# An FNet and SwiGLU block on one core: modulation's sums rearranged, one row block's load moved, and the last but one group's second products in seven instead of eight

## The chip, the core and the metric

The kernel runs on one core of a Trainium2 chip. The time is the device time of one execution, in microseconds (us). A run gives the median of several executions; beside it there is one profiled execution with a trace of each engine: TensorE (PE, its weight loads PEld), VectorE (DVE), ScalarE (ACT), GpSimd (POOL) and SyncE (SP).

## The reference

A row block of 2048 rows by 512 columns goes through a Fourier mixing layer and then a gated feed-forward layer, each behind a layer norm that is modulated by a conditioning vector c:

```python
mod = (_silu(c) @ w_mod).reshape(c.shape[0], 6, 1, -1)
sa, ca, ga, sb, cb, gb = (mod[:, 0], mod[:, 1], mod[:, 2], mod[:, 3], mod[:, 4], mod[:, 5])
h = _layernorm(x, axis=-1) * (1 + ca) + sa
x = x + ga * _A_ref(h, A_dft_seq_re, A_dft_seq_im, A_dft_hid_re, A_dft_hid_im)
h = _layernorm(x, axis=-1) * (1 + cb) + sb
x = x + gb * _B_ref(h, B_w1, B_w3, B_w2)
# _A_ref: y = Cr @ (h Wr) - Ci @ (h Wi);  _B_ref: (silu(h w1) * (h w3)) w2
```

## The kernel before

All matmuls on float32 data are made of splits: a tile is rounded to a high part (a copy on ScalarE), the rest is its low part (a subtraction on VectorE), and a product is three matmuls (high by high, high by low, low by high). `product` does these three.

**The start.** ScalarE and SP issue the first loads. The sums sa and ca of modulation come from `mod_scale` and `mod_sum`: the four parts of w_mod for one vector (tiles `wmr`; `wm[v, h][:, n]`, v = 1 for ca, 0 for sa) are scaled by silu(c) and added up on VectorE, the first of them scaled by ScalarE (`copy_by`), and four small matmuls by ones (`mod_sum`) sum them over the partitions. `mod_read` takes them out of PSUM, and then `modulate_rows` (tile `hm`) can begin on the first row block, which has been normalized (`norm_stats`, `norm_root` with a square root on ScalarE, `norm_inverse`, `norm_scale`) and transposed (`turn_rows`) by then. `keep_warm` issues matmuls that nobody reads; 25 of them stand between the last sum and the first real product. After the start, `arrange` orders tasks by a table of ranks and times, until the products over the sequence (line 750) begin.

**The feed-forward part.** The 1792 columns in the middle are seven groups g of 256, and the four column blocks t of 512 rows are two pairs: pair 0 is t = 0 and 2, pair 1 is t = 1 and 3. The products by w1 (called a) and w3 (called b) of one group and pair are done by Strassen's method in Winograd's form: seven units, a1 to a7 and b1 to b7 (`factor`), of six matmuls of 512 columns. From them come `v` = silu(a) times b and its split `hf`. The second products, by w2 (called y in the program's string of the order), are spread between the a and b units of the next group. For the groups in the list `SEVEN`, 0 to 4 of pair 1, they too are seven units (`seven_unit`, in the order 2, 5, 3, 1, 6, 7, 4), of six matmuls in two PSUM banks, 6 and 7; units 3, 6, 7 and 4 add to the banks of the unit before them, so each unit's banks have to be read before the next unit with the same banks begins. ScalarE reads them (`copy_by`, line 335, tile `y`, scaled by gb), and a transfer that POOL issues adds `y` (512 KB) to `sums` in DRAM. Such groups also need the sums of w2's quarters and their splits (`seven_jobs`: tiles `w2s`, `w2sh`, `w2sl`) and four differences of `v` (`seven_parts`). All other groups have eight units of six matmuls (`down_unit`).

Groups 5 and 6 of pair 1 come last. Their eight units each are `own`: VectorE adds the bank, scaled by gb, to the tile `xr` (line 1147), which `load_sums` has loaded from `sums` after group 4; after group 6 the result goes from `xr` to the output. Here `down_banks` are 6, 7, 0, 1 and 2 in turn. The order of the last units is a string, `body`, for each group; `behind(n, ...)` puts the splits some units later, `delayed` issues them ahead of a unit. Everything an engine gets, it does in the order of the program.

Of the kernel before, what the change touches and what calls it, by code (L numbers as in the profile page):

```python
# [12 lines left out]
OP = mybir.AluOpType  # L13
AX = mybir.AxisListType

P = 128
# [5 lines left out]
NT = S // N  # L22
ND = D // P
# [19 lines left out]
def folded(nc, pools, c, cp, wmr, wmc, x, xt, ctr, cti, wdr, wdi, w1, w3, w2, out):  # L43
# [155 lines left out]

    held = consts.tile([1, 1], F32, name="held")  # L200

    def load_x(k, other=nc.sync):
        if k >= NK // 2:
            nc.gpsimd.tensor_copy(held, wd[0][0:1, 1, 0:1].bitcast(F32))


        i, par = where(k)
        xz[k] = take(F32, "x")
        nc.sync.dma_start(xz[k][:, 0, :], x[i][par::2])
        if par:  # L210
# [27 lines left out]
    load_wm(0, 1, nc.sync)  # L238
    for dt in range(2):
        load_hid(dt, nc.sync)  # L240
    load_x(1)
    for dt in range(2, ND):
        load_hid(dt, nc.sync)
    for k in range(2, 4):
# [53 lines left out]

    mod_acc = [bank(5), bank(6)]

    def mod_scale(v, h):

        w, own = wm[v, 0][:, 0, :], wm[v, h]
        if h == 0:
            copy_by(w, w, sc[:, 0:1])
        for n in range(1 - h, 2):
            nc.vector.scalar_tensor_tensor(
                w, own[:, n, :], sc[:, 2 * h + n : 2 * h + n + 1], w, op0=OP.mult, op1=OP.add
            )

    def mod_sum(v):

        for dt in range(ND):
            nc.tensor.matmul(
                mod_acc[v][:, cols(dt)],
                hid_cols(wm[v, 0][:, 0, :], dt),
                onesf[:, :P],
                start=True,
                stop=True,
            )  # L320

    def mod_read(v):
# [11 lines left out]
    def copy_by(dst, src, by):  # L334
        nc.scalar.activation(dst, src, AF.Identity, scale=by)  # L335
# [789 lines left out]
    def down_unit(g, pair, t, d, key):  # L1125
        last = g == NG - 1

        own = pair == 1 and g >= NG - 2
        if not own and d % 2 == 0:
            ys[0] = take(F32, "y")  # L1130

        parts = 2 if own and last and (t, d) == (NT - 1, ND - 1) else 1
# [32 lines left out]
        if d == ND - 1:  # L1165
            for q in range(2):
                give(hf.pop((g, t, q)))
            if t == PAIRS[pair][1]:
                give_w(key)
            if pair == 1 and g == NG - 3:  # L1170
                load_sums(t)
# [51 lines left out]
    TO = {1: 0, 6: 0, 7: 0, 4: 0, 2: 1, 5: 2, 3: 2}  # L1223
    state, vs = {}, {}

    SEVEN = [(g, 1) for g in range(NG - 2)]
    ORDER7 = (2, 5, 3, 1, 6, 7, 4)
    LEFT7 = {1: "h0", 2: "h2", 4: "h3", 5: "s0", 6: "s1", 7: "s2", 3: "s3"}
    TO7 = {2: (0, 0), 5: (1, 1), 3: (0, 1), 1: (0, 0), 6: (0, 1), 7: (1, 1), 4: (1, 0)}
# [101 lines left out]
    def seven_unit(g, pair, n, key):  # L1331
        new = n in (1, 2, 5)
        if new:
            banks7[:] = [bank(6), bank(7)]
        y = take(F32, "y")
        which, k = TO7[n]
        t = PAIRS[pair][k]
        names = ("h", "l") if LEFT7[n][0] == "h" else ("sh", "sl")
        u = right7.pop(((g, pair), n))
        for e, to in enumerate(banks7):  # L1340
            at = int(LEFT7[n][1]) * HALF + e * P
            product(
                to,
                [flat(wuse[key][x])[:, at : at + P] for x in names],
                [u[:, b, :] for b in range(2)],
                new,
                True,
                not new,
            )
            d = 2 * which + e  # L1350
            copy_by(y[:, e, :], to, gb[:, d : d + 1])
        give(u)
        nc.gpsimd.dma_start(sums[t, which], y, accum_op=OP.add)  # L1353
        behind(4, lambda: give(y))
        if n == ORDER7[-1]:
            for x in wuse.pop(key).values():
                give(x)
            if g == NG - 3:
                for t in PAIRS[pair]:
                    load_sums(t)  # L1360
# [134 lines left out]
    }  # L1495
    seq_steps = []
    keep_warm(3)
    for side in range(2):
        norm_stats(0, side)
    norm_root(0)  # L1500
    norm_inverse(0)
    for side in range(2):
        norm_scale(0, side, "ACT" if side else "DVE")
        turn_rows(0, side)
    keep_warm(1)
    for v, h in ((1, 0), (1, 1), (0, 0)):
        mod_scale(v, h)
    mod_sum(1)
    copy(nought, zero[:, 0, :P])
    clear_z()  # L1510
    hid_begin(0)
    keep_warm(6, P)
    mod_scale(0, 1)
    mod_read(1)
    mod_sum(0)
    mod_read(0)


    at(10.0, "turn0.0", "turn0.1")
# [184 lines left out]
    def down(g, pair, *which):  # L1704
        key = which[-1]
        drain(lambda: (key, "l") in done, jobs)
        delayed()
        if (g, pair) in SEVEN:
            seven_unit(g, pair, *which)
        else:  # L1710
            down_unit(g, pair, *which)
        beside(1.36, USED["own" if pair == 1 and g >= NG - 2 else "y"])

    for w in ("w1", "w3"):
        load_w((w, 1))
# [36 lines left out]
    def unit(kind, i, n):  # L1752
# [23 lines left out]
        if (kind, n) == ("b", 3):  # L1776
# [9 lines left out]
            if (g, pair) in SEVEN:  # L1786
                seconds.extend((g, pair, n, ("w2", g, pair)) for n in ORDER7)
            else:
                for t in PAIRS[pair]:
                    seconds.extend((g, pair, t, d, ("w2", g, pair)) for d in range(ND))  # L1790
# [7 lines left out]
    for i in range(len(items)):  # L1798
# [834 lines left out]
```

## Time and profile before

| | us |
|---|---|
| median of 3 runs (lowest, highest) | 692.39 (691.91, 694.4) |
| the profiled execution: its own time | 690.63 |
| its span, first to last instruction | 688.8 |
| TensorE busy | 672.4 |
| VectorE busy | 586.8 |
| ScalarE busy | 451.2 |

A row of a timeline gives start and duration in us, the engine, the source line, the operation, the tile written and the tiles read, the shape and a count; in brackets stand the engine's idle time before it and what ended that. Times are from the first instruction. L335 is ScalarE's scaled copy, L100 a matmul of `product`, L87 a copy on ScalarE, L90, L93 and L96 VectorE's subtraction, addition and multiplication.

### The profile page before, as it was taken

What the parts mean: (1) busy time and instruction counts of PE and PEld (TensorE: products, weight loads), DVE (VectorE), ACT (ScalarE), POOL (GpSimd) and SP (SyncE); (2) the same over time, 40 slices, a digit from 0 to 9 for tenths busy, and PEclk for the clock granted to TensorE, in tenths of its full rate; (3) what the DMA queues carried; (4) which work ended last, traced back from release to release, by engine and by line L of the source; (5) the groups of instructions that cost most, each with busy time, mean ns of one, the idle gap of its engine ahead of it and who ended that gap; (6) DMA issues with size and microseconds to landing.
All of it is one profiled execution on the core that took longest, in us unless ns stands there. A gap on an engine that the chain in (4) does not pass through costs nothing.

```text
span 688.8 us, 9035 instructions
## 1 busy us (share of the span) xinstructions
PE 672.4 (98%) x3122; PEld 557.4 (81%) x3122; DVE 586.8 (85%) x945; ACT 451.2 (65%) x751; POOL 132.2 (19%) x156
## 2 busy tenths in 40 slices
PE   6999999999999999999999999999999999999996
PEld 4898788888888888888788888887887888888785
DVE  5999769998999987989997989787998979888465
ACT  4998956455343665663577767867687887877620
POOL 1320162543435000100101001011011112221100
PEclk9999999999999999999999999999999999999998
DMA  8740299787679440274767666475859998999713
GB/s 264 224 124 1 54 368 339 249 297 258 197 287 291 154 151 30 46 139 122 119 141 141 150 153 121 94 128 118 267 108 183 175 203 167 181 214 173 179 45 127
DMA packets 40837, 116.80 MB, mean 170 GB/s; under 512 B 5200, under 2 KB 5456, under 8 KB 40784
## 3 DMA queue, kind: packets, MB, share of 16 engines
q0 software_dynamic: 14512, 50.86, 36.9%
q1 hardware_dynamic: 25840, 63.98, 28.1%
q10 hardware_dynamic: 432, 1.31, 0.6%
q8 instruction: 26, 0.43, 0.3%
q14 instruction: 27, 0.22, 0.1%
HBM read 76.81 MB, written 41.42 MB: 172 GB/s over the span
## 4 chain that ended last, share of the span: by engine, by line
PE 84%; DVE 9%; ACT 4%; issue 1%; DMA 1%; SPq 0%; DVEq 0%; ACTq 0%
PE bank L100 54%; PE bank L750 26%; PE bank L559 2%; PE bank L598 1%; ACT hm L501 1%; DMA x<-in_x 1%; DVE xr L806 1%; DVE st L449 1%; PE bank L576 1%; DVE v L96 1%; DVE hl L90 0%; DVE ul L90 0%; DVE x L93 0%; ACT hh L87 0%; DVE w3s L90 0%
## 5 line engine op out<-in xcount | busy, mean ns | idle before, releaser
L100 PE MATMUL bank<-hf,w2h 128*128 128x512 f32 (+1 forms) x352 | 108.3, 389 | 0.0
L87 ACT ACTIVATE hf<-v 128x512 fp32r<-128x512 f32 x71 | 44.4, 631 | 66.7 <-DVE v L96 53.9
L335 ACT ACTIVATE y<-bank,gb 128x512 f32<-128x512 f32 x118 | 76.5, 682 | 3.9 <-PE bank L100 3.6
L100 PEld LDWEIGHTS bank<-hf,w2h 128*128 128x128 f32 x352 | 65.6, 188 | 15.4 <-ACT y L335 1.5
L1161 POOL DMA_DIRECT2D sum<-y x28 | 24.0, 857 | 240.7 <-ACT y L335 124.5
L100 PE MATMUL bank<-hf,w2l 128*128 128x512 f32 (+1 forms) x176 | 68.1, 387 | 0.0
L90 DVE TENSOR_TENSOR hf<-v,hf 128x512 fp32r<-128x512 f32 x71 | 48.7, 685 | 10.6 <-ACT hf L87 10.5
L1353 POOL DMA_DIRECT2D sum<-y x35 | 29.8, 852 | 128.3 <-ACT y L335 120.8
L87 ACT ACTIVATE x<-bank 128x512 f32<-128x512 f32 x72 | 41.7, 591 | 13.6 <-PE bank L100 12.7
L750 PE MATMUL bank<-d,uh 128*128 128x512 f32 x128 | 49.9, 390 | 0.0
L750 PE MATMUL bank<-l,us 128*128 128x512 f32 x128 | 49.9, 390 | 0.0
L750 PE MATMUL bank<-d,us 128*128 128x512 f32 x128 | 49.9, 390 | 0.0
L750 PE MATMUL bank<-bh,us 128*128 128x512 f32 x128 | 49.9, 390 | 0.0
L750 PE MATMUL bank<-bh,ul 128*128 128x512 f32 x128 | 49.8, 389 | 0.0
L750 PE MATMUL bank<-l,uh 128*128 128x512 f32 x128 | 49.8, 389 | 0.0
L170 POOL DMA_INDIRECT re<-in_ctr,mirror x32 | 35.7, 1115 | 66.6 <-ACT im L188 40.1
L170 POOL DMA_INDIRECT im<-in_cti,mirror x32 | 32.9, 1028 | 33.4 <-DVE l L90 8.9
L100 PEld LDWEIGHTS bank<-hf,w2l 128*128 128x128 f32 x176 | 33.1, 188 | 6.6
L93 DVE TENSOR_TENSOR v<-bank,x 128x512 f32<-128x512 f32 x36 | 24.7, 686 | 15.6 <-PE bank L100 14.0
L1245 ACT ACTIVATE v<-v 128x512 f32<-128x512 f32 x36 | 22.6, 629 | 22.7 <-DVE v L93 22.4
L93 DVE TENSOR_TENSOR x<-bank,x 128x512 f32<-128x512 f32 x36 | 24.7, 685 | 14.5 <-PE bank L100 13.7
L188 ACT ACTIVATE im<-l 128x512 f32<-128x512 f32 x16 | 10.1, 632 | 32.4 <-DVE d L93 15.5
(260 smaller groups left out, 1922.4 us busy)
## 6 DMA issues: line engine op xcount, KB each, us to landing
sum<-y POOLq DMA_DIRECT2D x63, 512.0 KB, 5.7
w<-in_w SPq DMA_DIRECT2D x42, 512.0 KB, 4.8
re<-in_ctr SPq DMA_DIRECT2D x32, 256.0 KB, 5.8
im<-in_cti SPq DMA_DIRECT2D x32, 256.0 KB, 5.3
wmc<-in_wmc SPq DMA_DIRECT2D x8, 512.0 KB, 7.2
sum<-xr SPq DMA_DIRECT2D x8, 512.0 KB, 5.6
x<-in_x SPq DMA_DIRECT2D x11, 256.0 KB, 4.5
xr<-in_xt SPq DMA_DIRECT2D x8, 256.0 KB, 7.1
```

Of the source, the lines that this page charges most:

```text
L87: nc.scalar.activation(dst, src, AF.Copy, scale=scale)
L90: nc.vector.tensor_tensor(out=dst, in0=a, in1=b, op=OP.subtract)
L93: nc.vector.tensor_tensor(out=dst, in0=a, in1=b, op=OP.add)
L100: nc.tensor.matmul(acc, lhs[a], rhs[b], start=first and n == 0, stop=last and n == len(PASSES) - 1, skip_group_check=more,)
L170: nc.gpsimd.indirect_dma_start(dst, None, rows, bass.IndirectOffsetOnAxis(ap=at, axis=0))
L188: nc.scalar.activation(to, src.bitcast(F32), AF.Square, accum_out=chk[:, kind, KINDS.index(m), n : n + 1],)
L335: nc.scalar.activation(dst, src, AF.Identity, scale=by)
L559: nc.tensor.matmul(halves(hb[k])[:, m, :], sides((hh, hl)[a][k])[:, dt, m, :], wu[dt][:, b, m, :], start=False, stop=dt % 2 == 1 and n == ...
L750: nc.tensor.matmul(acc[what, e], lhs, rhs, start=begin and i == 0, stop=(end or (turn and what == "x")) and i == len(terms) - 1, skip_grou ...
L1161: nc.gpsimd.dma_start(sums[t, d // 2], y, accum_op=OP.add)
L1245: behind(k != 0 or q == 0, lambda: nc.scalar.activation(v, src, AF.Silu))
L1353: nc.gpsimd.dma_start(sums[t, which], y, accum_op=OP.add)
```

## The change

Three things are changed. At the start, ca's first copy and first add, and the zeroing copies, stand ahead of the layer norm's square root and its scaling; sa is summed in two parts, by two sets of four matmuls that add up in PSUM, with a matmul by zeros ahead of them to set the bank to zero (`mod_begin`), so that one add on VectorE is replaced by a copy on ScalarE. Second, the load of row block 1 is issued by ScalarE, behind the scaled copies, and not by SP. Third, group 5 of pair 1 joins `SEVEN`: its second products are seven units that are read by ScalarE and added by transfers, to `xr` in SBUF; the string of the last group's order is adapted, and the last group's eight units take the places of t = 3 ahead of the last two of t = 1.

```diff
@@ load_x and the first loads
-    def load_x(k, other=nc.sync):
+    def load_x(k, other=nc.sync, one=nc.sync):
...
-        nc.sync.dma_start(xz[k][:, 0, :], x[i][par::2])
+        one.dma_start(xz[k][:, 0, :], x[i][par::2])
...
-    load_x(1)
@@ modulation
-    def mod_scale(v, h):
-
-        w, own = wm[v, 0][:, 0, :], wm[v, h]
-        if h == 0:
-            copy_by(w, w, sc[:, 0:1])
-        for n in range(1 - h, 2):
-            nc.vector.scalar_tensor_tensor(
-                w, own[:, n, :], sc[:, 2 * h + n : 2 * h + n + 1], w, op0=OP.mult, op1=OP.add
-            )
+    def mod_copy(v, h, n):
+        w = wm[v, h][:, n, :]
+        copy_by(w, w, sc[:, 2 * h + n : 2 * h + n + 1])
+
+    def mod_add(v, h, n):
+        w, own = wm[v, 0][:, 0, :], wm[v, h]
+        nc.vector.scalar_tensor_tensor(
+            w, own[:, n, :], sc[:, 2 * h + n : 2 * h + n + 1], w, op0=OP.mult, op1=OP.add
+        )
+
+    def mod_begin():
+        nc.tensor.matmul(
+            mod_acc[0], zero[:, 0, :P], onesf, start=True, stop=False, skip_group_check=True
+        )
...
-    def mod_sum(v):
+    def mod_sum(v, h=0, apart=False):
...
-                hid_cols(wm[v, 0][:, 0, :], dt),
+                hid_cols(wm[v, h][:, 0, :], dt),
                 onesf[:, :P],
-                start=True,
-                stop=True,
+                start=not apart,
+                stop=not apart or h == 0,
+                skip_group_check=apart,
@@ the start's order
     keep_warm(3)
+    copy(nought, zero[:, 0, :P])
+    clear_z()
     for side in range(2):
         norm_stats(0, side)
+    mod_copy(1, 0, 0)
     norm_root(0)
+    mod_add(1, 0, 1)
     norm_inverse(0)
...
-    keep_warm(1)
-    for v, h in ((1, 0), (1, 1), (0, 0)):
-        mod_scale(v, h)
+    mod_begin()
+    mod_add(1, 1, 0)
+    mod_copy(0, 0, 0)
+    mod_add(1, 1, 1)
+    mod_copy(0, 1, 0)
+    load_x(1, nc.scalar, nc.scalar)
     mod_sum(1)
-    copy(nought, zero[:, 0, :P])
-    clear_z()
+    mod_add(0, 0, 1)
+    mod_sum(0, 1, True)
+    mod_add(0, 1, 1)
+    keep_warm(1, P)
+    mod_sum(0, 0, True)
+    mod_read(1)
+    mod_read(0)
     hid_begin(0)
-    keep_warm(6, P)
-    mod_scale(0, 1)
-    mod_read(1)
-    mod_sum(0)
-    mod_read(0)
@@ the second products
-        own = pair == 1 and g >= NG - 2
+        own = pair == 1 and g == NG - 1
...
-    SEVEN = [(g, 1) for g in range(NG - 2)]
+    SEVEN = [(g, 1) for g in range(NG - 1)]
...
-        nc.gpsimd.dma_start(sums[t, which], y, accum_op=OP.add)
+        to = xr[t][which] if g == NG - 2 else sums[t, which]
+        nc.gpsimd.dma_start(to, y, accum_op=OP.add)
...
+                if not more:
+                    places = places[:2] + places[4:] + places[2:4]
...
-            body = "a6 a5 b1 a7 a3 b2 a4 y b6 y b5 y b7 y b4 y y b3 y y y y y y y y y y"
+            body = "a6 a5 b1 a7 a3 b2 y a4 y b6 y b5 y b7 y b4 y b3 y y y y y y y y y"
```

How the change moves instructions is shown at three places; after a name stand a bank's or buffer's number and a counter.

**ScalarE at the start**, before: silu(c) (`sc`), the square root (`rs`) with its table load, the scaling of the first row block's second half, and two scaled copies.

```order
L286 ACT_TABLE_LOAD
L286 ACTIVATE sc_145<-cc_84 128x4
L454 ACT_TABLE_LOAD
L454 ACTIVATE rs_0_162<-mv_0_161,eps_128 128x2
L468 ACTIVATE x_1_87<-x_1_87,rs_0_162 128x512
L335 ACTIVATE wmr_2_90<-wmr_2_90,sc_145 128x512
L335 ACTIVATE wmr_4_94<-wmr_4_94,sc_145 128x512
L87 ACTIVATE nought_155<-zero_13_140 128x128
```

The same place of ScalarE after the change:

```order
L285 ACT_TABLE_LOAD
L285 ACTIVATE sc_142<-cc_84 128x4
L87 ACTIVATE nought_152<-zero_12_137 128x128
L87 ACTIVATE z_17_153<-zero_12_137 128x1024
L340 ACTIVATE wmr_2_90<-wmr_2_90,sc_142 128x512
L459 ACT_TABLE_LOAD
L459 ACTIVATE rs_0_161<-mv_0_160,eps_125 128x2
L473 ACTIVATE x_1_87<-x_1_87,rs_0_161 128x512
L340 ACTIVATE wmr_4_94<-wmr_4_94,sc_142 128x512
L340 ACTIVATE wmr_5_96<-wmr_5_96,sc_142 128x512
L209 DMA x_20_190<-in_x 128x1x512
L211 DMA x_20_190<-in_x 128x1x512
```

The second table load and the square root now stand behind the first scaled copy, and two DMA issues behind the last.

**ScalarE where group 5's b units end and group 6's a units begin**, before: w3sh is the high part of group 6's w3 sums, hf_960 a split of group 5's v, the y are evictions of group 4's units, x_963 and v_964 results of a1 and a2.

```order
L87 ACTIVATE w3sh_956_5829<-w3s_951_5809 128x1024
L87 ACTIVATE x_958_5838<-bank5_957_5831 128x512
L87 ACTIVATE hf_960_5850<-v_916_5606 128x512
L335 ACTIVATE y_961_5852<-bank6_952_5815,gb_152 128x512
L335 ACTIVATE y_961_5852<-bank7_953_5816,gb_152 128x512
L87 ACTIVATE x_963_5870<-bank0_962_5863 128x512
L1245 ACTIVATE v_964_5871<-v_964_5871 128x512
L335 ACTIVATE y_968_5885<-bank6_952_5815,gb_152 128x512
```

After the change ScalarE has there:

```order
L87 ACTIVATE x_958_5837<-bank5_957_5830 128x512
L87 ACTIVATE hf_960_5852<-v_916_5605 128x512
L340 ACTIVATE y_961_5854<-bank6_952_5814,gb_149 128x512
L340 ACTIVATE y_961_5854<-bank7_953_5815,gb_149 128x512
L87 ACTIVATE w3sh_963_5866<-w3s_959_5839 128x1024
L87 ACTIVATE x_965_5876<-bank0_964_5869 128x512
L1251 ACTIVATE v_966_5877<-v_966_5877 128x512
L340 ACTIVATE y_971_5893<-bank6_952_5814,gb_149 128x512
```

w3sh has moved from ahead of hf_960 to behind the two y. VectorE, after the change, has at the same place (w3l and w3sl are the low parts of group 6's w3 and of its sums; the rows ahead of these are the sums and splits of w2, which are new):

```order
L90 TENSOR_TENSOR w3s_959_5839<-w3_934_5728,w3s_959_5839 128x256
L93 TENSOR_TENSOR x_958_5837<-bank3_943_5765,x_958_5837 128x512
L96 TENSOR_TENSOR v_916_5605<-v_916_5605,x_958_5837 128x512
L90 TENSOR_TENSOR w3l_962_5864<-w3_934_5728,w3h_956_5828 128x1024
L90 TENSOR_TENSOR hf_960_5852<-v_916_5605,hf_960_5852 128x512
L90 TENSOR_TENSOR w3sl_969_5882<-w3s_959_5839,w3sh_963_5866 128x1024
L93 TENSOR_TENSOR v_966_5877<-bank1_970_5884,x_965_5876 128x512
```

Before, w3l and w3sl stood ahead of x_958 and v_916; now they stand behind them, and w3sl ahead of v_966.

**ScalarE and TensorE at the end.** The last activations of ScalarE were, before, an x and three splits hf; after the change they are:

```order
L87 ACTIVATE hf_1004_6109<-v_967_5878 128x512
L340 ACTIVATE y_1005_6111<-bank6_999_6069,gb_149 128x512
L340 ACTIVATE y_1005_6111<-bank7_1000_6070,gb_149 128x512
L87 ACTIVATE hf_1006_6150<-v_966_5877 128x512
L340 ACTIVATE y_1007_6152<-bank6_999_6069,gb_149 128x512
L340 ACTIVATE y_1007_6152<-bank7_1000_6070,gb_149 128x512
```

hf_1006 is the split of the v that b3 ends, y_1007 the eviction of unit 4. TensorE's unit 4 and the first unit of the last group stand so after the change:

```order
L100 MATMUL bank6_999_6069<-hf_985_5991,w2h_947_5793 128x512 x2
L100 MATMUL bank6_999_6069<-hf_985_5991,w2l_950_5809 128x512
L100 MATMUL bank7_1000_6070<-hf_985_5991,w2h_947_5793 128x512 x2
L100 MATMUL bank7_1000_6070<-hf_985_5991,w2l_950_5809 128x512
L100 MATMUL bank7_1008_6163<-hf_989_6008,w2h_987_6003 128x512 x2
L100 MATMUL bank7_1008_6163<-hf_989_6008,w2l_988_6005 128x512
```

bank7_1000 and bank7_1008 are the same PSUM bank, one after the other.

More of the change, by code (lines that the diff above doesn't have):

```diff
@@ L1126, in down_unit @@
         last = g == NG - 1
-        own = pair == 1 and g >= NG - 2
+        own = pair == 1 and g == NG - 1
         if not own and d % 2 == 0:
             ys[0] = take(F32, "y")
-        parts = 2 if own and last and (t, d) == (NT - 1, ND - 1) else 1
+        final = (t, d) == ((PAIRS[1][0] if own else PAIRS[pair][1]), ND - 1)
+        parts = 2 if own and final else 1
         for n in range(parts):
@@ L1167, in down_unit @@
                 give(hf.pop((g, t, q)))
-            if t == PAIRS[pair][1]:
+            if final:
                 give_w(key)
@@ L1711, in down @@
             down_unit(g, pair, *which)
-        beside(1.36, USED["own" if pair == 1 and g >= NG - 2 else "y"])
+        beside(1.36, USED["own" if pair == 1 and g == NG - 1 else "y"])
     for w in ("w1", "w3"):
@@ L1788, in unit @@
             else:
-                for t in PAIRS[pair]:
-                    seconds.extend((g, pair, t, d, ("w2", g, pair)) for d in range(ND))
+                t0, t1 = PAIRS[pair]
+                places = [(t, d) for t in (t0, t1) for d in range(ND)]
+                if not more:
+                    places = places[:2] + places[4:] + places[2:4]
+                seconds.extend((g, pair, t, d, ("w2", g, pair)) for t, d in places)
         if (kind, n) == ("b", 6) and more and early_w3(i):
```

## The prediction

> **What bounds the kernel now.** First the busy shares and the chain of work that ended last.
>
> ```profile
> PE 672.4 (98%) x3122; PEld 557.4 (81%) x3122; DVE 586.8 (85%) x945; ACT 451.2 (65%) x751; POOL 132.2 (19%) x156
> PE 84%; DVE 9%; ACT 4%; issue 1%; DMA 1%; SPq 0%; DVEq 0%; ACTq 0%
> 86.65 174.32 PE bank L750 x768
> ```
>
> TensorE is busy for 98% of the span and is 84% of the chain; from 86.65 us on the chain is TensorE alone for 174 us. So what counts is TensorE's issue time: matmuls taken out of it, and waits put into it. Other engines matter only in the first 86 us, where the chain runs through them, and where TensorE waits for them. The timeline of TensorE late in the program gives the pace:
>
> ```profile
> 639.40 0.39 PE L100 MATMUL bank<-th,w3h 128*128 128x512 f32 x1
> 640.53 0.39 PE L100 MATMUL bank<-th,w3l 128*128 128x512 f32 x1
> 640.93 0.73 PE L100 MATMUL bank<-hf,w2h 128*128 128x512 f32 x2
> 642.42 0.39 PE L100 MATMUL bank<-h2h,w3sh 128*128 128x512 f32 x1
> ```
>
> The first and sixth matmul of one unit start 1.13 us apart, so a matmul costs 0.226 us and a unit of six 1.36 us (its listed 0.39 us is overlapped). The next unit could have begun at 640.76; it began 0.17 late, and took 1.49 us: a restart after a wait costs another 0.13. That is a second product waiting for its bank, and the point that the change presses on.
>
> **The start.** Its rows, from the timeline and (the second one) the DMA issues:
>
> ```profile
> 1.41 1.16 ACTq L220 DMA_DIRECT2D wmr<-in_wmr  x2
> wmr<-in_wmr ACTq DMA_DIRECT2D x2, 512.0 KB, 6.9
> 2.60 4.51 PE L281 MATMUL bank<-tmp 128*128 128x512 f32 x6 [2.60 <-DVE tmp L275]
> 2.61 1.28 ACT L286 ACT_TABLE_LOAD   x1 [2.61 <-issue]
> 3.90 0.20 ACT L286 ACTIVATE sc<-cc 128x4 f32<-128x4 f32 x1
> 4.12 1.28 ACT L454 ACT_TABLE_LOAD   x1
> 7.50 0.30 ACT L454 ACTIVATE rs<-mv,eps 128x2 f32<-128x2 f32 x1 [2.09 <-DVE mv L450]
> 8.23 0.55 DVE L470 TENSOR_SCALAR x<-x,rs 128x512 f32<-128x512 f32 x1
> 9.95 1.02 PE L281 MATMUL bank<-tmp 128*128 128x512 f32 x2
> 10.07 0.72 ACT L335 ACTIVATE wmr<-wmr,sc 128x512 f32<-128x512 f32 x1 [0.42 <-DMA wmr<-in_wmr]
> 10.47 1.54 DVE L307 SCALAR_TENSOR_TENSOR wmr<-wmr,sc,wmr 128x512 f32<-128x512 f32 x2
> 12.06 1.21 PE L314 MATMUL bank<-tmp,wmr 128*128 128x128 f32 x8 [1.09 <-DVE wmr L307]
> 13.03 0.48 PE L549 MATMUL bank<-z,nought 128*128 128x512 f32 x1
> 15.62 5.75 PE L281 MATMUL bank<-tmp 128*128 128x128 f32 x50
> 16.02 1.02 ACT L501 ACTIVATE hm<-bank,mod 128x256 f32<-128x256 f32 x2 [1.94 <-DVE mod L324]
> 21.82 0.51 PE L559 MATMUL bank<-wu,hh 128*128 128x256 f32 x2 [0.45 <-ACT hh L87]
> ```
>
> Before, ScalarE loads the Sqrt table at 4.12, in idle time. Now the table load stands behind the first scaled copy of w_mod, and that copy waits for its DMA. The two ScalarE DMAs took 6.9 us on average; the second, issued at about 2.0, ended the copy's wait at 10.07, so took 8.0; the first then took 5.8 and landed at 1.41 + 5.8 = 7.2. Copy 0.72, table load 1.28: Sqrt at 9.2 instead of 7.50, **1.7 us later**. VectorE's scaling starts 0.73 after Sqrt (8.23 - 7.50): 9.93, ends 10.48. Now only two adds (0.77 each, 1.54 for two) stand before the first sum: 12.02, and TensorE starts it at 12.07, where it started before (12.06). What was gained by moving adds forward is spent on the table load.
>
> From there TensorE sets the pace. One sum takes 0.97 (12.06 to 13.03). Before, the two sums with the product by zeros and 12 filler passes between them ended at 15.62, where the 50 passes begin. Now come three sums and one filler matmul (two passes of 5.75/50): 12.07 + 3 x 0.97 + 0.23 = 15.21. VectorE's last two adds end at 12.02 + 1.54 = 13.56, under that. The mod values, and so hm on ScalarE, come **0.41 us sooner** (15.6 for 16.02). The 25 filler matmuls then end at 15.21 + 0.23 (the product by zeros) + 5.75 = 21.2, and the first real product is due at 21.82 - 0.41 = 21.41: they still fit. Beyond it the order of all engines up to the last two groups is as before, and no load stands on the chain there, so I carry the 0.41 to 86.65 and to the end. Its ends: 0 (absorbed on the way), and 2.1, if the table load cost nothing (1.7 more). The second row block's two DMA issues now cost ScalarE 1.16 (as at 1.41), between the copies' end at about 12.0 and hm at 15.6, where two casts of 0.42 are all else: covered. If that cover went, hm would be late by the rest of 1.16. SP is free of them; nothing was seen waiting for SP's loads of the third and fourth weight part, so I count nothing.
>
> The Trainium skill, ScalarE: Activation LUTs, What ACT_TABLE_LOAD costs, adds a drain of 1.38 us to each switch of 1.28. Here the load at 2.61 ends at 3.89 and the next activation starts at 3.90: the trace shows no drain. By the page Sqrt would come at 10.6 and the start would lose about 1.0 instead of gaining 0.41, and the sum below would be 4.5 instead of 3.15.
>
> **The last two groups.** Removed: 48 matmuls become 42, 6 x 0.226 = **-1.36 us**. Also removed are eight VectorE additions from PSUM; added are 14 ScalarE evictions, seven POOL transfers into xr, splits and sums of w2, and four differences. None of these is on TensorE's path by itself; what matters is where TensorE waits for an eviction. I follow three places.
>
> ```profile
> 630.87 0.42 DVE L93 TENSOR_TENSOR w3s<-w 128x256 f32<-128x256 f32 x1
> 632.33 0.68 DVE L90 TENSOR_TENSOR hf<-v,hf 128x512 fp32r<-128x512 f32 x1
> 632.93 1.21 DVE L90 TENSOR_TENSOR w3l<-w,w3h 128x1024 fp32r<-128x1024 f32 x1
> 634.07 1.22 DVE L90 TENSOR_TENSOR w3sl<-w3s,w3sh 128x1024 fp32r<-128x1024 f32 x1
> 635.92 0.69 DVE L96 TENSOR_TENSOR v<-v,x 128x512 f32<-128x512 f32 x1
> 632.95 1.06 ACT L87 ACTIVATE w3sh<-w3s 128x1024 fp32r<-128x1024 f32 x1
> 636.64 0.63 ACT L87 ACTIVATE hf<-v 128x512 fp32r<-128x512 f32 x1 [2.15 <-DVE v L96]
> 637.18 1.25 ACT L335 ACTIVATE y<-bank,gb 128x512 f32<-128x512 f32 x2
> 638.32 0.59 ACT L87 ACTIVATE x<-bank 128x512 f32<-128x512 f32 x1
> 638.95 0.69 DVE L93 TENSOR_TENSOR v<-bank,x 128x512 f32<-128x512 f32 x1 [0.95 <-ACT x L87]
> 639.67 0.63 ACT L1245 ACTIVATE v<-v 128x512 f32<-128x512 f32 x1 [0.76 <-DVE v L93]
> 640.21 1.25 ACT L335 ACTIVATE y<-bank,gb 128x512 f32<-128x512 f32 x2
> ```
>
> *First wait, at 640.93.* Ahead of the v at 635.92, VectorE loses w3l and w3sl (2 x 1.14, from 632.93 to 634.07) and gains the four w2 sums (1.46, as 630.87 to 632.33) and w2sl (1.14): v comes 0.32 later, at 636.24, and ends at 636.94; hf on ScalarE at 636.97, y y at 637.51. Behind them now stands w3sh, which stood ahead before: 638.65 to 639.71. VectorE's w3sl waits for it: 639.74, and the v of 638.95 is queued behind w3sl (1.14): 640.88. Silu follows 0.72 later (639.67 - 638.95): 641.60, y y 0.54 later: 642.14, and TensorE 0.72 after that (640.93 - 640.21): 642.86. **+1.92 us.** Its ends: 0.32 if the wait for w3sh were hidden, and 1.92; every link has a row, so I take 1.92.
>
> *Two small ones.* ScalarE now evicts the new units behind an hf that waits for VectorE. From the end C of b2: v ends at C+1.62, hf, then y from C+2.19 (the steps of the next fence), free at C+2.91; unit 5 is due two units later, C+2.72: 0.19 and a restart of 0.13. Behind b7 the same with 0.07 more of VectorE: 0.25 + 0.13. Together **+0.70**, ends 0 and 0.70.
>
> *The last wait.* TensorE, VectorE and ScalarE around the last factor unit, b3:
>
> ```profile
> 666.90 0.39 PE L100 MATMUL bank<-h2h,w3sh 128*128 128x512 f32 x1
> 668.46 0.69 DVE L93 TENSOR_TENSOR x<-bank,x 128x512 f32<-128x512 f32 x1 [0.61 <-PE bank L100]
> 669.91 0.63 ACT L87 ACTIVATE hf<-v 128x512 fp32r<-128x512 f32 x1 [4.11 <-DVE v L96]
> ```
>
> b3 ends at B = 668.26; hf starts at B+1.65. Before, nothing followed it on ScalarE. Now the eviction of unit 4 does, and the next unit, the first of the last group, is written into bank 7 again, half of what is evicted. y from B+1.65+0.54 = B+2.19, both halves done 1.25 later, B+3.44, TensorE 0.09 after (0.72 - 0.63): B+3.53. It was due after unit 4, B+1.36: a wait of 2.17 and a restart, **+2.30**. If the eviction went first, it would still be 1.05 (0.20 + 0.63 + 0.09 + 0.13). I take 2.30, by ScalarE's order.
>
> **Sum:** -0.41 - 1.36 + 1.92 + 0.70 + 2.30 = **+3.15 us**. The profiled execution's own time is 690.63 us (span 688.8): 693.8. The three runs lie higher, with a median of 692.39, so on their scale 695.5.
>
> **Rivals.** *Evictions don't hold TensorE* (ScalarE is idle 35% of the span): only the savings stay, -1.8 us, 690.6. Against it: both late units before, and the bank order. 10%. *The transfers into xr land late*, slower: no row shows an accumulation into SBUF; into DRAM it takes
>
> ```profile
> sum<-y POOLq DMA_DIRECT2D x63, 512.0 KB, 5.7
> ```
>
> Unit 4's is issued as the last group starts and needed six units and its own later: 7 x 1.36 + 0.2 = 9.7 us. It decides from there; at 12 us, twice the row, it costs 2.3: 697.8. 6%. *TensorE's clock falls at the start*, slower: its pause from 7.11 grows from 1.8 to 3.5 us. Its first matmuls took 0.75 each (4.51/6), later ones 0.51 (1.02/2); three sums at 1.47 times 0.97 cost 1.4: 696.9. 7%. By the Trainium skill, TensorE: Matmul & The Clock Gate, Part 1, the clock halves after an idle window of about 3.4 us that runs freely; 1.8 us without a loss agrees, and a pause of 3.5 seldom holds a whole window.
>
> **Numbers.** The forecast has 77%, its own range 694.2 to 696.8. 0.5%, 3.46 us, is about what a measurement here can tell from no change; 3.15 lies close under it. Of the 77 some 29 fall above it: slower 29 + 6 + 7 = 42%; within 0.5% the other 48 and 8 of the first rival's 10, 56%; faster 2%, for the first rival with a start gain of 2.1. The range, 692.8 to 697.2, leaves out the first rival and the top.
>
> **What would show it.** Sqrt at 9.2 and hm at 15.6; TensorE idle for some 1.8 us ahead of the unit after -b4, released by y; an idle of about 2.2 us ahead of the first unit of the last group, released by y; no wait of VectorE for a DMA at xr. No idle at these two places would make it wrong.

## The result, and the profile after

The change makes the kernel slower, by more than was forecast:

| | median, us | runs | ratio to before (95% interval) |
|---|---|---|---|
| before | 691.67 | 6 (690.8 to 694.4) | |
| after | 699.28 | 6 (696.89 to 700.83) | 1.0097 (1.0079 to 1.0116) |

The ratio is +6.7 us (5.5 to 8.0). The profiled execution of after took 700.83 us, its span is 699.0. Busy shares and chain on the page of after:

```profile
PE 677.1 (97%) x3114; PEld 559.3 (80%) x3114; DVE 587.7 (84%) x948; ACT 463.1 (66%) x770; POOL 138.7 (20%) x163
PE 76%; DVE 12%; ACT 5%; DMA 4%; issue 2%; SPq 0%; ACTq 0%; DVEq 0%
```

TensorE has eight matmuls fewer, is busy for 4.7 us more, and its share of the chain fell from 84% to 76%, while DMA's rose from 1% to 4%. The timeline of the start, after:

```profile
2.60 5.49 PE L280 MATMUL bank<-tmp 128*128 128x512 f32 x6 [2.60 <-DVE tmp L274]
8.77 0.72 ACT L340 ACTIVATE wmr<-wmr,sc 128x512 f32<-128x512 f32 x1 [3.49 <-DMA wmr<-in_wmr]
9.51 1.28 ACT L459 ACT_TABLE_LOAD   x1
10.80 0.29 ACT L459 ACTIVATE rs<-mv,eps 128x2 f32<-128x2 f32 x1
12.22 1.10 PE L490 MATMUL bank<-ident,x 128*128 128x128 f32 x4 [4.13 <-DVE x L475]
13.97 1.91 PE L311 MATMUL bank<-tmp,zero 128*128 128x512 f32 x2
15.67 3.18 PE L318 MATMUL bank<-tmp,wmr 128*128 128x128 f32 x16
15.81 0.54 ACTq L209 DMA_DIRECT2D x<-in_x  x1
16.80 0.54 ACTq L211 DMA_DIRECT2D x<-in_x  x1
17.39 0.72 ACT L87 ACTIVATE wu<-w 128x256 fp32r<-128x256 f32 x2 [3.82 <-DMA w<-in_wdr]
20.25 1.02 ACT L506 ACTIVATE hm<-bank,mod 128x256 f32<-128x256 f32 x2 [2.14 <-DVE mod L329]
```

The square root comes at 10.80 (before 7.50), TensorE has paused for 4.13 us (1.81), four transposes take 1.10 (0.72), and hm comes at 20.25: 4.2 us later, not 0.4 sooner. The windows of the same trace give the granted clock (the column ahead of the last two, between POOL and the DMA share):

```profile
8.00:10.00 2.00, 0.09 (x1) 0.00 (x0) 0.48 (x1) 1.21 (x2) 0.00 (x0) 1.00 1.03 405
12.00:14.00 2.00, 1.78 (x9) 1.81 (x10) 1.96 (x4) 1.57 (x3) 0.00 (x0) 0.50 0.97 237
16.00:18.00 2.00, 2.00 (x11) 2.00 (x11) 0.16 (x1) 0.61 (x2) 0.00 (x0) 0.50 0.85 199
20.00:22.00 2.00, 2.00 (x20) 1.96 (x19) 1.94 (x9) 1.75 (x5) 0.00 (x0) 1.00 1.09 261
```

The clock is half, by finer windows from 11.4 to 18.2 us. At the end, first behind -b4, then ahead of the last group:

```profile
643.75 1.06 ACT L87 ACTIVATE w3sh<-w3s 128x1024 fp32r<-128x1024 f32 x1
644.84 1.23 DVE L90 TENSOR_TENSOR w3sl<-w3s,w3sh 128x1024 fp32r<-128x1024 f32 x1 [1.06 <-ACT w3sh L87]
645.98 0.69 DVE L93 TENSOR_TENSOR v<-bank,x 128x512 f32<-128x512 f32 x1
647.24 1.25 ACT L340 ACTIVATE y<-bank,gb 128x512 f32<-128x512 f32 x2
647.96 0.74 PE L100 MATMUL bank<-hf,w2h 128*128 128x512 f32 x2 [1.59 <-ACT y L340]
...
677.76 0.63 ACT L87 ACTIVATE hf<-v 128x512 fp32r<-128x512 f32 x1 [1.99 <-DVE v L96]
678.30 1.25 ACT L340 ACTIVATE y<-bank,gb 128x512 f32<-128x512 f32 x2
679.60 0.73 PE L100 MATMUL bank<-hf,w2h 128*128 128x512 f32 x2 [1.97 <-ACT y L340]
692.51 0.48 DVE L1153 SCALAR_TENSOR_TENSOR xr<-bank,gb,xr 128x256 f32<-128x256 f32 x1 [0.23 <-PE bank L100]
```

Both waits stand where the prediction put them, with the chain of releasers that it named (v behind w3sl behind w3sh; y behind hf). But from the last group's first matmul to the last addition it takes 12.9 us, and 11.2 before (670.98 to 682.13). Windows and the page's DMA issues:

```profile
681.00:682.00 1.00, 1.00 (x4) 0.81 (x3) 0.43 (x2) 0.00 (x0) 0.00 (x0) 0.50 1.01 184
...
xr<-y POOLq DMA_DIRECT2D x7, 512.0 KB, 5.5
```

The clock is half again, by finer windows from 680.4 to 683.8. The transfers into xr land in 5.5 us, under the 9.7 from which they would matter.

### The profile page after: what moved, and what is told of

It is laid out like the page before. It is cut to its first block, busy times and chain, and to the rows that moved or that the text cites. A ratio compares the mean times of both kernels' runs of the same rounds, so it can differ in the third digit from the quotient of the medians.

```text
span 699.0 us, 9050 instructions
## 1 busy us (share of the span) xinstructions
PE 677.1 (97%) x3114; PEld 559.3 (80%) x3114; DVE 587.7 (84%) x948; ACT 463.1 (66%) x770; POOL 138.7 (20%) x163
## 4 chain that ended last, share of the span: by engine, by line
PE 76%; DVE 12%; ACT 5%; DMA 4%; issue 2%; SPq 0%; ACTq 0%; DVEq 0%
PE bank L100 52%; PE bank L755 19%; DMA wmc<-in_wmc 2%; PE bank L564 2%; PE bank L603 1%; DMA wmr<-in_wmr 1%; DVE v L96 1%; DVE x L93 1%; ACT y L340 1%; DVE d L93 1%; PE bank L490 1%; ACT hm L506 1%; DVE xr L811 1%; DVE ul L90 1%; PE bank L318 1%
## 5 line engine op out<-in xcount | busy, mean ns | idle before, releaser
L100 PE MATMUL bank<-hf,w2h 128*128 128x512 f32 (+1 forms) x332 | 103.6, 394 | 3.6 <-ACT y L340 3.6
L340 ACT ACTIVATE y<-bank,gb 128x512 f32<-128x512 f32 x132 | 85.7, 682 | 4.1 <-PE bank L100 3.6
L87 ACT ACTIVATE hf<-v 128x512 fp32r<-128x512 f32 x74 | 46.1, 631 | 59.5 <-DVE v L96 48.2
L100 PEld LDWEIGHTS bank<-hf,w2h 128*128 128x128 f32 x332 | 62.5, 190 | 18.7 <-ACT y L340 5.4
L100 PE MATMUL bank<-hf,w2l 128*128 128x512 f32 (+1 forms) x166 | 64.7, 390 | 0.0
L90 DVE TENSOR_TENSOR hf<-v,hf 128x512 fp32r<-128x512 f32 x74 | 50.6, 686 | 11.4 <-ACT hf L87 11.3
L100 PEld LDWEIGHTS bank<-hf,w2l 128*128 128x128 f32 x166 | 31.6, 190 | 6.5
```

Of the source, the lines that this page charges most:

```text
L87: nc.scalar.activation(dst, src, AF.Copy, scale=scale)
L90: nc.vector.tensor_tensor(out=dst, in0=a, in1=b, op=OP.subtract)
L100: nc.tensor.matmul(acc, lhs[a], rhs[b], start=first and n == 0, stop=last and n == len(PASSES) - 1, skip_group_check=more,)
```

## The experiments

Ratios are to the kernel before on the same chip.

| kernel | median, us | ratio to before (95% interval) |
|---|---|---|
| 1 end alone | 695.31 | 1.0052 (1.0032 to 1.0071) |
| 2 start alone | 693.75 | 1.0021 (1.0009 to 1.0033) |
| 3 after, root first | 697.84 | 1.0086 (1.0071 to 1.0102) |
| 4 after, pause at the start filled | 699.51 | 1.0112 (1.0092 to 1.0131) |
| 5 row block 1 alone | 696.75 | 1.0068 (1.0052 to 1.0085) |
| 6 after, root first, row block 1 on SP | 696.96 | 1.0073 (1.0048 to 1.0097) |
| 7 after, free banks | 696.05 | 1.0066 (1.0047 to 1.0084) |
| 8 after, free banks, w2 and test later | 695.27 | 1.0052 (1.0034 to 1.0070) |
| 9 start, root first | 694.91 | 1.0032 (1.0014 to 1.0051) |
| 10 start, row block 1 on SP | 693.77 | 1.0021 (1.0006 to 1.0036) |
| 11 start, both put back | 692.73 | 1.0006 (0.9990 to 1.0022) |
| 12 before, mended end | 692.09 | 0.9996 (0.9983 to 1.0009) |
| 13 after, pause at the end filled | 698.06 | 1.0081 (1.0065 to 1.0096) |
| 14 after, beside 13 | 698.70 | 1.0100 (1.0079 to 1.0121) |

What their timelines show of the start: when the root of row block 0 comes, how long TensorE pauses ahead of the transposes, for how long its clock is half in or behind that pause, when row block 1's second half is issued, when the first hm comes, and the first product over the sequence (83.72 before).

| trace | root | pause | half clock | issue | hm | first product | it less hm |
|---|---|---|---|---|---|---|---|
| before | 7.50 | 1.81 | 0 | SP 12.81 | 16.02 | 83.72 | 67.70 |
| 1 (the start of before) | 8.61 | 2.87 | 3.4 | SP 12.90 | 17.13 | 84.84 | 67.71 |
| after | 10.80 | 4.13 | 6.8 | ACT 16.80 | 20.25 | 87.95 | 67.70 |
| 14 (after again) | 10.34 | 3.67 | 3.4 | ACT 16.24 | 18.45 | 86.66 | 68.21 |
| 2 | 10.36 | 3.69 | 3.4 | ACT 16.38 | 18.70 | 86.94 | 68.24 |
| 3 | 9.02 | 2.35 | 3.4 | ACT 16.45 | 17.78 | 86.86 | 69.08 |
| 4 | 8.95 | 0.15 | 0 | ACT 15.97 | 17.19 | 87.22 | 70.03 |
| 9 | 7.46 | 0.86 | 0 | ACT 16.62 | 17.84 | 87.91 | 70.07 |
| 10 | 9.26 | 3.72 | 6.8 | SP 12.83 | 18.38 | 86.08 | 67.70 |
| 11 | 8.50 | 2.90 | 3.4 | SP 12.54 | 16.61 | 84.31 | 67.70 |

With row block 1 on SP the first product follows hm by 67.70 or 67.71 us in these rows (by 68.33 in the trace of 6, 15.71 to 84.04). With ScalarE issuing it, the first product comes at 86.7 to 88.0 in these rows, whatever hm does.

### Halves of the change: 1 and 2

Kernel 1 is before with only the end's part, kernel 2 before with only the start's two.

> The kernel before, with only the third part of the change (group 5 of pair 1 in seven products, the last group's new order). Theory: the waits for evictions cost 1.9 + 0.4 + 2.1, less 1.4 for six matmuls fewer, in all +3.5 us on 691.7, so 695.2; and where the clock of TensorE falls after the pause ahead of the last group, as in the trace after the change (half clock from 680.4 to 683.8 us), 1.7 more, 696.9. Rival: the waits at the end came only from the start's delay, since it shifts transfers against the matmuls: then 691.7 or under, by up to 1.4.

> The kernel before, with only the first two parts of the change (modulation's sums sooner, row block 1 on ScalarE's queue). Theory: the first hm comes at 20.2 instead of 16.0 us and 0.9 more is lost in the products over the sequence, so +4.2 to +5.1 on 691.7: 695.9 to 696.8. Rival: the late start is made up for later, as the tasks have slack before 86 us, and the time is that of before, 691.7.

Kernel 1: +3.6 us (0.0052 x 692.06). From the first product by w1 to the last addition its trace takes 262.01 to 686.94, 424.93 us, and before 260.81 to 682.13, 421.32: **+3.61, predicted +3.56**. The first theory holds for the end, and there was no half clock in its last group. Kernel 2 lost 1.5 us in its median, between the theory's 4.2 or more and the rival's nothing; its profiled execution is its slowest. The losses are real and separate, and the start's differs from execution to execution. So does the start of before: in the trace of 1, which has that start, row block 0 landed 1.1 us later than in the trace of before (its statistics begin at 6.87 instead of 5.76), TensorE's pause grew to 2.87 us, the clock fell, and the first product came at 84.84 instead of 83.72.

### What holds the start: 3, 4, 5 and 6

3 and 6 put edits back in after; 4 fills the pause; 5 is before with row block 1 alone moved.

```diff
@@ 3 (and 6)
-    mod_copy(1, 0, 0)
     norm_root(0)
-    mod_add(1, 0, 1)
     norm_inverse(0)
     for side in range(2):
         norm_scale(0, side, "ACT" if side else "DVE")
         turn_rows(0, side)
+    mod_copy(1, 0, 0)
+    mod_add(1, 0, 1)
@@ 4
-    keep_warm(3)
+    keep_warm(5)
+    keep_warm(4, P)
@@ 5, in before
-    load_x(1)
...
         mod_scale(v, h)
+    load_x(1, nc.scalar, nc.scalar)
@@ 6, beside 3's edit
+    load_x(1)
...
-    load_x(1, nc.scalar, nc.scalar)
```

> The kernel after the change, with ca's first scaled copy and first add put back behind the layer norm's scaling. Theory: the square root's table load is in ScalarE's idle time again, the root at 7.5 us, TensorE pauses for under 2 us, its clock stays at 1.00, and the first hm comes at 15 to 16.5 us; the time falls by 4 to 5 us from 699.3, to 694.3 to 695.3. Rival: the parts of w_mod land too late whatever stands ahead (8.7 and 11 us), and hm stays at 18.5 or later: 697.5 or more.

> The kernel after the change, with two filler matmuls of 512 columns and four of 128 columns more ahead of the transposes, which fill most of TensorE's pause from 8.1 to 12.2 us. Theory that the clock is most of it: the square root stays at 10.8 us and the transposes at 12.2, but transposes, the matmuls by zeros and the sums run at full pace, the first hm comes at 17.0 to 17.5 and the time falls by 3 us, to 696.3. Rival that the clock does not matter there, because the sums wait for VectorE and the table load: hm at 19.5 or later, and the time within 1 us of 699.3.

> The kernel before, with only the second part of the change: row block 1 loaded by ScalarE behind the scaled copies. Theory: ScalarE's issue of the second half waits until an earlier transfer of the hidden weights has landed, so that the half lands at about 22 us instead of 18; the square root of row block 1 comes at 22.9 to 23.3 instead of 20.3, and the first product over the sequence 67.7 - 4.3 us behind that, at 86.3 to 86.9 instead of 83.7: +2.5 to +3 us on the time of before. Rival: the two issues cost ScalarE only their 1.1 us, beside other work, and the time is that of before within 0.5 us.

> The kernel after the change, with both put back: the first scaled copy and add behind the layer norm's scaling, and row block 1 on SP's queue. Theory that two separate floors hold the start, the late first hm and the late row block 1: with both gone the first hm comes at 16 to 17.8 us and the first product over the sequence 67.7 us later, at 83.7 to 85.5, and only the end's losses stay: 695 to 696. Rival that row block 1 has no part in it: as with the copy alone put back, the first product at 86.9 and 697.8.

4 was the telling miss: its clock stayed at 1.00 up to 24.0 us, hm came 3.1 us sooner than in after, as that theory said, and the time was no better. (Of the 3.1 us, 1.85 are luck: the first part of w_mod landed sooner in this trace, and the root came at 8.95 and not at 10.80.) Its timeline:

```profile
8.95 0.30 ACT L459 ACTIVATE rs<-mv,eps 128x2 f32<-128x2 f32 x1
14.92 0.56 ACTq L209 DMA_DIRECT2D x<-in_x  x1
15.50 0.35 DVE L329 TENSOR_SCALAR mod<-bank 128x1 f32<-128x1 f32 x4 [1.95 <-PE bank L318]
15.97 0.54 ACTq L211 DMA_DIRECT2D x<-in_x  x1
16.56 0.72 ACT L87 ACTIVATE wu<-w 128x256 fp32r<-128x256 f32 x2 [4.84 <-DMA w<-in_wdr]
17.19 1.00 ACT L506 ACTIVATE hm<-bank,mod 128x256 f32<-128x256 f32 x2
21.95 0.69 DVE L454 BATCH_NORM_STATS2 st<-x 128x6 f32<-128x512 f32 x1 [1.84 <-DMA x<-in_x]
22.89 0.29 ACT L459 ACTIVATE rs<-mv,eps 128x2 f32<-128x2 f32 x1 [1.29 <-DVE mv L455]
24.37 0.80 PE L564 MATMUL bank<-wu,hh 128*128 128x256 f32 x2 [3.09 <-ACT hh L87]
```

mod is ready at 15.9, but ScalarE stands at its DMA issues until 16.5, then does two casts queued behind them: hm at 17.19. Row block 1 lands at 21.95, its root comes at 22.89 (20.34 before), and TensorE waits 3.09 us ahead of the first real product. At the end of that pause the clock fell after all (windows of the same trace):

```profile
22.00:24.00 2.00, 0.00 (x0) 0.00 (x0) 1.97 (x5) 1.11 (x4) 0.00 (x0) 1.00 1.04 380
24.00:27.00 3.00, 2.63 (x12) 2.56 (x13) 2.93 (x10) 2.98 (x7) 0.00 (x0) 0.51 0.73 270
```

So 4 kept full clock for the sums, not for the whole start. From the first real product to the first one over the sequence it takes 62.85 us, and 62.17 to 62.19 in 2, 3, 7, 8, 13 and 14, where row block 1 is late as well and the clock isn't half at that place: some 0.7 us. Why the issues come so late, the chain of waits of kernel 2 shows (start, us, what):

```profile
12.41 3.95 DMA w<-in_wdr
16.36 0.02 issue
16.38 5.93 DMA x<-in_x
22.31 0.02 issue
22.33 0.71 DVE st L454
```

The second half's issue waits until a transfer of the hidden weights, issued at 12.41, has landed. Why the program has it wait for this transfer, the trace doesn't show. In before, the loads of row block 1 stood on SP, with only more loads behind them. On ScalarE hm stands behind them.

5 shows the part alone at +4.7 us (0.0068 x 691.48), more than expected, since in before the zeroing copies are queued behind the two issues (hm at 22.11 there):

```profile
15.78 0.54 ACTq L211 DMA_DIRECT2D x<-in_x  x1
16.37 0.31 ACT L87 ACTIVATE nought<-zero 128x128 fp32r<-128x128 f32 x1 [4.53 <-DMA w<-in_wdi]
17.68 0.80 PE L548 MATMUL bank<-z,nought 128*128 128x512 f32 x1 [2.66 <-ACT z L87]
```

3 lies 0.8 us below after by the ratios (1.0086 and 1.0097), and its time is in its rival's range, but neither account fits: hm came at 17.78, sooner than the rival's 18.5 and later than the theory's 16.5. Row block 0 landed late in this trace, so the root came at 9.02 and the clock fell; and what set the first product, at 86.86, was row block 1, whose statistics waited 1.50 us for its DMA and began at 22.26. 6 missed by its median: its trace has hm at 15.71 and the first product at 84.04, as the theory of two floors says, but TensorE then waited 1.4 us once for an addition to xr on VectorE in the sequence stage, and its runs spread over 5 us (693.99 to 699.01). It settles nothing by time. So the three that follow have the end of before.

### The start without the end: 9, 10 and 11

They are kernel 2 with 3's edit, with row block 1 back on SP, and with both.

> The kernel before with the start's parts of the change, but ca's first scaled copy and add behind the layer norm's scaling (row block 1 stays on ScalarE's queue). Theory of two floors: the first hm comes at 16 to 17.8 us, yet the first product over the sequence stays at 86 to 87 us, held by row block 1, whose root comes at about 23; time 693 to 694, hardly less than the 693.75 of the start alone. Rival that the root's place is the whole loss: within 0.4 of before, 691.5 to 692.

> The kernel before with the start's parts of the change, but row block 1 on SP's queue as before (the first scaled copy stays ahead of the root). Theory of two floors: the first hm still comes at 17.5 to 20 us, behind table load and half clock, and the first product over the sequence 67.7 later, 85.2 to 87.9; time 692.5 to 694. Rival that row block 1 is the whole loss: 691.5 to 692.

> The kernel before with the start's parts of the change, and both put back: what is left is that sa is summed in two parts and the zeroing copies stand early. Theory: the first hm comes at 15.6 to 16.8 us, the first product over the sequence at 83.3 to 84.5, and the time is that of before or up to 0.4 under it: 691.1 to 692. Rival that the sum in two parts itself costs time: 692.5 or more.

Neither edit alone takes the loss away (694.91 and 693.77, with 693.75 for kernel 2); both together do, to within the uncertainty (1.0006). By the medians alone that would be weak: the intervals of 10 and 11 overlap, and 11's median of 692.73 lies in its rival's range (on its chip before took 692.05), so a small cost of the sum in two parts isn't excluded. 11 isn't under before: in its trace row block 0 landed a microsecond later than in the trace of before (root at 8.50) and the clock fell.

The traces carry the theory of **two floors**: the later of two chains sets the start, so mending one uncovers the other. In all sixteen traces (before, after and 1 to 14) the first real product begins 1.48 us behind the square root of row block 1. In nine the load of row block 1 stands on ScalarE behind the rearranged sums. In eight of them the statistics of row block 1 wait 0.61 to 2.05 us for its DMA and begin at 21.95 to 23.50 (18.11 in before). In the ninth, that of after, they begin at 22.34 without such a wait, 2.09 behind hm, as in before (16.02 and 18.11). So hm held the start there, and the late row block stood close below.

9 is above its theory's 693 to 694. Row block 1 made TensorE pause for 3.71 us ahead of the first real product, and the clock fell there, from 24.8 us for 3.4 us; the rest of the way to the first product over the sequence took 63.04 us. A floor that is uncovered brings a pause, and here the pause brought half clock.

### The end: 7, 8 and 12

```diff
@@ 7
-            down_banks[:] = [6, 7, 0, 1, 2]
+            down_banks[:] = [0, 1, 2, 6, 7]
+            turn[1] = 0
@@ 8, beside 7's edit
-        if (kind, n) == ("b", 2):
+        if (kind, n) == ("b", 2) and (g, pair) != (NG - 2, 1):
...
             weight_jobs(i + 1, "w3")
+            if (g, pair) == (NG - 2, 1):
+                seven_jobs(("w2", g, pair))
...
-                if (i, len(seconds)) == (len(items) - 1, 9):
+                if (i, len(seconds)) == (len(items) - 1, 6):
                     judge()
@@ 12: the start of before, 8's edits, but seven_jobs in the last group:
+        if not more and (kind, n) == ("a", 2):
+            seven_jobs(("w2", NG - 2, 1))
```

> The kernel after the change, with the last group's units in banks 0, 1, 2, 6, 7 in turn, so that its first unit finds a bank that nobody has to read. Theory: the pause of 2.0 us ahead of it goes, but the third unit of the group needs the low part of the hf that b3 ends, which VectorE makes behind the 3 us of reductions of the final test (680.66 in the trace after): 1.2 us come back there, and 0.9 are left; where the clock no longer falls behind the pause, 1.7 more: 696.7 to 698.4. Rival: the transfers into xr are the real limit, and the first addition to xr waits for them at once: 699.3.

> As the run with free banks, and also w2's splits of group 5 made behind those of group 6's w3, and the final test's reductions three units later. Theory: the pause ahead of the last group goes without a new one (-2.1), that behind -b4 falls from 2.0 to about 0.4 (-1.6), and the clock does not fall (-1.7 in runs where it did): 694 to 695.6. Rival: other waits for evictions take their place and less than 2 us are gained: 697.3 or more.

> The kernel before with only the third part of the change, the last group's units in banks 0, 1, 2, 6, 7, the final test's reductions three units later, and w2's splits of group 5 made in the last group, behind its second unit. Theory: no pause ahead of the last group, one of some 0.5 us behind -b4, the two small ones of 0.3 and 0.4 as before, six matmuls fewer (-1.36): the stretch from the first product by w1 to the last addition takes 421.0 to 421.6 us (421.3 before), and the time is that of before within 0.4: 691.2 to 692. Rival: ScalarE and VectorE are full in the last two groups, a wait that is taken away there comes back at the next unit, and the stretch takes 422.3 or more: 692.7 or more.

The stretch from the first product by w1 to the last addition: 424.93 us in 1, 423.85 in 7, 422.35 in 8, 420.90 in 12, 421.32 before. In 7 the pause ahead of the last group is gone, and the new wait stands where it was expected, in the group's third unit, for the split that VectorE makes behind the reductions of the final test (`judge`, on the checks of the weights):

```profile
678.56 0.67 DVE L90 TENSOR_TENSOR hf<-v,hf 128x512 fp32r<-128x512 f32 x1
679.28 0.50 PE L100 MATMUL bank<-hf,w2h 128*128 128x512 f32 x1 [0.80 <-DVE hf L90]
```

In 8 it is gone, and the wait behind -b4 is down to 0.25 us, but 1.61 us stand now at the product by w2 that comes just ahead of -b4. VectorE has w3sl there, which waits for w3sh, and the four sums of w2 ahead of the x and v; ScalarE's hf waits for v, and y stands behind hf:

```profile
637.43 1.23 DVE L90 TENSOR_TENSOR w3sl<-w3s,w3sh 128x1024 fp32r<-128x1024 f32 x1 [0.88 <-ACT w3sh L87]
641.49 0.63 ACT L87 ACTIVATE hf<-v 128x512 fp32r<-128x512 f32 x1 [2.65 <-DVE v L96]
642.74 0.73 PE L100 MATMUL bank<-hf,w2sh 128*128 128x512 f32 x2 [1.61 <-ACT y L340]
```

So 8's median, 695.27, is in the theory's range, but its stretch shrank by 2.6 us from that of 1 and not by the 3.7 that the theory has for the two pauses: the rival's new wait came too.

12 moves w2's splits to where nothing waits: 0.4 us under before in that stretch, and the same time in the median. It beats after, and it doesn't beat before: what six matmuls save (1.36), the small waits that are left take for the most part.

### Is half clock at the end part of the loss: 13 and 14

```diff
+            if own and (t, d, n) == (PAIRS[1][0], 0, 0):
+                filler = bank(0)
+                for _ in range(7):
+                    nc.tensor.matmul(filler, wuse[key][0][:, 0, cols(0)], hf[g, t, 0][:, 0, :], start=True, stop=True)
```

> The kernel after the change, with seven matmuls that nobody reads (into the free bank 0) in TensorE's pause ahead of the last group. They take nothing of the wait itself. Theory that half clock behind this pause is part of the loss: the last group's units run at full pace in every execution, from their first matmul to the last addition 11.3 us as against 12.9 in the trace after, and the median falls by 0.8 to 1.7 us under that of the change run beside it. Rival that the clock falls there only now and then: no difference over 0.5 us between the two medians.

> The kernel after the change itself, run beside the one with the pause filled, so that their medians and clocks are compared on one chip. Theory: 698 to 700, as before, and a mean granted clock lower by about 0.002 than with the pause filled (one stretch of 3.4 us at half clock is 0.5 x 3.4 / 697 = 0.0024). Rival that the change's runs were slow by their chip alone: 696 or less.

The medians differ by 0.64 us, between the theory's 0.8 to 1.7 and the rival's 0.5 at most, and the mean clocks not at all (0.9942 in both, over the executions). In the trace of 14, TensorE pauses 1.97 us ahead of the last group, and the group takes 677.43 to 688.73, 11.3 us, at full clock. So half clock at the end comes now and then: 1.6 us in the trace after and in that of 4, none in those of 1, 3, 6 and 14, which have the same pause. The fall isn't the rule, and what it adds to the median isn't settled.

## Why the prediction was wrong

**The end was right.** The wait behind -b4: predicted +1.92; the first matmul behind it is 7.03 us later than before (647.96 for 640.93), 5.10 of which were there already at the unit b7 (635.94 for 630.84): +1.93. The last wait: predicted 2.17 and a restart of 0.13, measured 2.13 and the restart (due at 677.47, 1.36 behind the unit at 676.11; begun at 679.60). The two small ones stand at 661.98 and 673.26 in the trace of after: with their restarts 0.73 for 0.70. All together +3.61, in 1, for +3.56. The first rival (evictions don't hold TensorE) and the second (xr lands late) fell. The unit b7 before and after, and the unit ahead of the last group after:

```profile
630.84 0.39 PE L100 MATMUL bank<-th,w3sh 128*128 128x512 f32 x1
635.94 0.39 PE L100 MATMUL bank<-th,w3sh 128*128 128x512 f32 x1
676.11 0.61 PE L100 MATMUL bank<-hf,w2h 128*128 128x512 f32 x2
```

**The start failed: "-0.41" should have been +1.5 in the median, and +2.9 to +4.2 in the traces of after.** Three steps of it:

1. "Covered": the two DMA issues were priced at their 1.16 us on ScalarE and put at 12.0. They stand at 15.8 and 16.8, since an issue has a wait of its own. What is queued behind them on ScalarE can be late (hm began 1.7 us behind the last read of mod in 4 and 2.5 in 9, and 0.2 in before), and in eight of the nine traces the statistics of the row block wait for its DMA: this floor alone puts the first product over the sequence at about 86.6 or later, 2.9 behind before. The view of waits of SP's queue in the trace of before, from 0 to 20 us, has the warning (engine, line, what it waited for, us in all, times, longest):

```profile
SPq L231 <- DMA wmr<-in_wmr: 3.2, 4, 1.6
```

   Issues on SP wait for transfers that went ahead of them, and only loads stand behind these.
2. "7.2" for the first part of w_mod is right for the trace of before, where the quickest of these transfers took 5.8 us; it doesn't hold from trace to trace. Behind the change's start the scaled copy began between 6.91 (in 4) and 8.77 us (after). The table load behind it was right: 9.51 + 1.28 = 10.79, and the root at 10.80. The 1.38 us of drain in the Trainium skill, ScalarE: Activation LUTs, What ACT_TABLE_LOAD costs, are again not seen. That the root came close to the 10.6 us of that reckoning is chance: the copy ahead of it began 1.6 late.
3. The clock was a rival at 7%, for a pause of 3.5 us. It fell in all eleven traces with a pause of 2.35 us or more ahead of the transposes, and in none of the five with 1.81 or less. From the root of row block 0 to the last read of mod it takes 6.55 us in 4, without a fall, 7.9 to 8.2 in 2, 7, 8, 13 and 14 with 3.4 us of half clock, and 8.93 and 9.26 in 10 and after with 6.8. So the rival's price of 1.4 fits one stretch, and two cost 2.4 to 2.7. The prediction had 6.21 without a fall (15.41 less 9.2). By its own rows it should have had more, since it left the transposes and mod_begin off the path to the first sum: in 4 that sum begins at 12.26, behind mod_begin, and VectorE's adds had ended at 11.68.

In the trace of after, hm at 20.25 for 15.6 is 1.60 from the second step, 2.71 from the clock and 0.34 from the rest of that path; the first step was hidden below it. In 14, the same kernel, the clock was half for 3.4 us only, and the first step set the start. Together they are two chains of nearly one length, and I followed only one of them.

**The sum.** Start alone 1.45 and end alone 3.60 are 5.05 of 6.7 us; the intervals of the three ratios leave room for the difference. In the traces of before and 14 it is closed: first product +2.94 (86.66 for 83.72), end +3.66, together 6.6; their times differ by 6.65. Open stays why TensorE waits once in the sequence stage in some traces and not in others, with one and the same start (after: 0.62 us; 7 and 8: none):

```profile
135.04 0.47 PE L755 MATMUL bank<-bh,us 128*128 128x512 f32 x1 [0.62 <-DVE xr L811]
```

## What to carry to other kernels

A DMA issue moved to a computing engine brings its own wait with it: look up what the issue waited for on the old queue, and ask what stands behind it on the new one. Where two chains end close together, undo edits one at a time and both at once; one at a time showed no gain here. When products are taken out by a scheme whose partial results must be evicted in order, count the waits at each bank first: here they cost 5.0 us to save 1.4.

## What was not expected of the hardware

TensorE's half clock came in stretches of 3.4 us or twice that, behind every pause of 2.35 us or more after the first matmul: eleven ahead of the transposes, 2.66 us in the trace of 5 (17.68, above), and 3.09 and 3.71 us ahead of the first real product in 4 and 9. It didn't come behind pauses of 1.81 us or less, nor behind one of 2.07 us (13, at 25.93). The fall has no fixed distance from the pause: in 10 it came at 9.1 us, within a pause that ended at 10.68; in 3 at 11.6, 1.2 us behind one that ended at 10.44. That fits a window of about 3.4 us that runs freely (the Trainium skill, TensorE: Matmul & The Clock Gate, Part 1). By the page the clock falls after at least one idle window; here pauses shorter than a window sufficed. A pause of 1.97 us did it in two of six traces, which fits a window that the pause falls into or straddles by chance.
